# Weight narrowing on dense buffers, w_out's forms in w_in's ring, and both halves of the later batches' scores in one PSUM bank

## The chip, the cores and the metric

The kernel runs on one core of a Trainium2 chip. Its time is device microseconds (us) for one execution, taken as the median of several runs; the profile is of one further execution. Five engines run in parallel, each in its own order of instructions: TensorE (PE, with its weight loads shown apart as PEld), VectorE (DVE), ScalarE (ACT), GpSimd (POOL) and SyncE (SP), which here issues all DMAs. Matmuls write into PSUM, which has eight banks of 512 float32 columns for each of 128 partitions; everything else lives in SBUF.

## The reference

Channel attention for four batches, and a feed-forward network behind it:

```
B, N, C = 4, 6080, 256;  d_ff = 2048
qn = q / (norm(q, axis=1) + 1e-6);  kn = k / (norm(k, axis=1) + 1e-6)
s  = kn.transpose(0, 2, 1) @ qn / tau            # (B, 256, 256)
a  = exp(s - max);  a /= a.sum(-1) + 1e-9
x  = (v @ a).reshape(B * N, C)                   # 24320 tokens
h  = x @ w_in;  g = 0.5 * h * (1 + erf(h / sqrt(2)));  out = g @ w_out
```

Inputs are float32; the two weight matrices arrive as float64, which the kernel sees as pairs of 32-bit words.

## The kernel before, in words

The attention matrix is multiplied into w_in for each batch, so that a batch's tokens go through two matmul layers only. Every large product is made in a split form: each operand is a high part in a rounded 32-bit type (float32r) and a low part that is the rest, and three matmuls (high by high, low by high, high by low) are added in PSUM. Both layers also use a Strassen-like scheme of seven products of quarter blocks in the place of eight, for which sums and differences ("forms") of the weights and of the tokens are made.

**The stages.** (1) The scores of batch 0 in plain float32. (2) Eight rounds of `pair_out` and `plain_products` over the first pair of chunks of batch 0, while the remaining weights are narrowed from float64. (3) 184 steps, one for each chunk of up to 512 tokens and each of four groups of 512 hidden columns. A step runs seven products into the banks pa, pb, px and pz (`do`, L903 to L905), gelu on ACT twice (once rounded into `his`, L933, once whole into `gs`, L930), the low part on DVE into `los` (L936, L954), and the products with w_out of the step before it (L1020 to L1022 and L1036 to L1038) into the four banks po0 to po3.

**The scores of batches 1 to 3** are made inside the steps of the batch before. Every third step holds a "burst": four blocks of 128 tokens of k and q, already split into `hl`, are multiplied for the two halves m of the 256 k channels. In `burst` (L470) a half takes the whole spare bank: 512 columns in one pass hold k's high part by q's high part in columns 0 to 255 and by q's low part in columns 256 to 511, and a second pass of 256 columns adds k's low part by q's high part. `burst_sum` (L480) adds the bank's 512 columns to the running sum `sacc` in SBUF, once for each half; `softmax` (L623) adds the two halves of `sacc` together at its start (L636). There are 34 bursts. The first eight blocks of batch 1 go through `qk_fill` at the start.

**Narrowing** (`narrow`, L518) turns 512 pairs of words for each partition into a high and a low float32r array. The two words of a pair lie next to each other, so each 32-bit half is read with a step of two. L532 clamps the upper words and writes them back in place; L534 squares them on ACT; L537 and L539 shift the exponent bits, the second one again in place; L541 masks small values; L544 writes a power of two into the upper words; L545 multiplies the lower words by it; L547 (ACT), L548 and L549 make the high and the low part. Of the sixteen units five are narrowed in the first 70 us and eleven in stage 2, on two scratch tiles in turn, `kqc` and `osb`.

**w_out's forms** (`wo_forms`, `wo_adds`, `wo_hi`, `wo_lo`, L586 to L615) are made once for each of the four groups, in the first four steps: four sums into `osb` (L598), four more (L601 to L604), the high part of these on ACT (L608) and the low part on DVE (L612), in two pieces. One piece is written into `kqc`; the other goes into the front half of the same `osb` tile. Both are sent to DRAM by DMA (L614, L615) and read back later. There is one `osb` tile, so the next group's sums wait until the DMA has read it.

**What sets the order.** PE's order is written out by hand. ACT's, DVE's and SP's is set when the kernel is built by `Order` (L79): a list planner with a fixed price for each instruction runs the program 24 times on paper and keeps the order with the earliest end. Any change of an instruction, a buffer or a wait can move others far from it. Each engine then runs strictly in that order: an instruction that waits holds up everything behind it.

## Time and profile before

| | |
|---|---|
| median of 3 runs | 2061.69 us (2061.46 to 2065.83) |
| the profiled execution's own time | 2062.65 us |
| its span, first to last instruction | 2060.9 us |
| PE, PEld, DVE, ACT busy | 99%, 95%, 90%, 79% |
| weight loads and matmuls | 15958 each |

A matmul of 256 columns stays in the array for 275 ns, but the next one starts after 0.11 us, so "busy" says only that PE had work in flight. Lost time on PE shows in two ways: as idle time before a matmul, with what ended it, and as a granted clock under 1. Line numbers are those of the kernel before; "gs<-px" is the tile written and the tile read, and `p` is the tile p5, whose number the profile leaves out.

### The profile page before, as it was taken

How to read it: one execution, taken by the hardware profiler on the slowest of the kernel's cores; microseconds unless marked ns; L12 is line 12 of the kernel's file. 1: busy time of each engine (PE TensorE's matmuls, PEld its weight loads, DVE VectorE, ACT ScalarE, POOL GpSimd, SP SyncE). 2: the span in 40 equal slices, each digit the busy share in tenths (PEclk: the TensorE clock that was granted, in tenths of full speed). 3: DMA queues.
4: the chain of work that ended last, by engine and by line, in shares of the span. 5: the costliest groups of instructions: out<-in, count | busy, mean ns of one | idle time of the engine just before them, and what ended most of it. 6: DMA issues, size and time to landing. Idle time of an engine off the chain costs nothing.

```text
span 2060.9 us, 40753 instructions
## 1 busy us (share of the span) xinstructions
PE 2032.2 (99%) x15958; PEld 1962.3 (95%) x15958; DVE 1857.9 (90%) x2733; ACT 1620.7 (79%) x2720; POOL 1.3 (0%) x8
## 2 busy tenths in 40 slices
PE   8899999999999999999999999999999999999999
PEld 7778999999999999999999999999999999999999
DVE  6899899899899989999989999999998998898897
ACT  6666788888888888888988877777787777777776
POOL 0000000000000000000000000000000000000000
PEclk9999999999999999999999999999999999999999
DMA  9556687877787778687678666666556566566664
GB/s 376 177 187 220 225 277 239 270 262 258 245 298 253 244 252 273 223 279 257 225 267 267 206 225 225 215 211 213 198 185 224 177 200 214 189 202 206 199 196 166
DMA packets 153808, 475.31 MB, mean 231 GB/s; under 512 B 16016, under 2 KB 26256, under 8 KB 153104
## 3 DMA queue, kind: packets, MB, share of 16 engines
q1 hardware_dynamic: 153616, 472.71, 68.3%
q8 instruction: 125, 2.05, 0.4%
q14 instruction: 67, 0.55, 0.1%
HBM read 435.16 MB, written 37.49 MB: 229 GB/s over the span
## 4 chain that ended last, share of the span: by engine, by line
PE 87%; DVE 6%; DMA 3%; ACT 2%; issue 1%; SPq 0%; DVEq 0%; ACTq 0%
PE po L1038 10%; PE po L1037 10%; PE po L1036 10%; PE pb L903 5%; PE pb L904 5%; PE pb L905 5%; PE pa L903 5%; PE pa L904 5%; PE pa L905 5%; PE po L1020 4%; PE po L1022 4%; PE po L1021 4%; DMA raw<-qk 2%; PE pz L904 2%; PE pz L905 2%; PE pz L903 2%
## 5 line engine op out<-in xcount | busy, mean ns | idle before, releaser
L1038 PE MATMUL po<-los,wo 128*128 128x256 f32 (+1 forms) x1890 | 520.3, 275 | 0.8 <-DVE los L954 0.8
L1036 PE MATMUL po<-his,wo 128*128 128x256 f32 (+1 forms) x1890 | 520.4, 275 | 0.0
L1037 PE MATMUL po<-his,wo 128*128 128x256 f32 (+1 forms) x1890 | 519.9, 275 | 0.0
L936 DVE TENSOR_TENSOR los<-gs,his 128x512 fp32r<-128x512 f32 (+1 forms) x601 | 407.0, 682 | 67.9 <-ACT gs L930 53.4
L1036 PEld LDWEIGHTS po<-his,wo 128*128 128x128 f32 x1890 | 362.7, 192 | 1.9
L1038 PEld LDWEIGHTS po<-los,wo 128*128 128x128 f32 x1890 | 362.9, 192 | 1.3 <-DVE los L954 1.2
L1037 PEld LDWEIGHTS po<-his,wo 128*128 128x128 f32 x1890 | 362.9, 192 | 0.5
L954 DVE TENSOR_TENSOR los<-gs,his 128x1024 fp32r<-128x1024 f32 (+1 forms) x270 | 326.6, 1210 | 18.2 <-ACT his L950 16.6
L950 ACT CAST his<-gs 128x1024 fp32r<-128x1024 f32 (+1 forms) x270 | 281.2, 1043 | 75.3 <-DVE gs L947 73.2
L903 PE MATMUL pa<-vhi,wl 128*128 128x256 f32 (+1 forms) x920 | 253.3, 275 | 4.7 <-DVE pz L917 4.4
L903 PE MATMUL pb<-vhi,wl 128*128 128x256 f32 (+1 forms) x920 | 253.6, 276 | 3.1 <-ACT gs L930 1.3
L904 PE MATMUL pa<-vhi,wh 128*128 128x256 f32 (+1 forms) x920 | 253.2, 275 | 0.0
L905 PE MATMUL pa<-vlo,wh 128*128 128x256 f32 (+1 forms) x920 | 253.2, 275 | 0.0
L905 PE MATMUL pb<-vlo,wh 128*128 128x256 f32 (+1 forms) x920 | 253.1, 275 | 0.0
L904 PE MATMUL pb<-vhi,wh 128*128 128x256 f32 (+1 forms) x920 | 253.1, 275 | 0.0
L943 DVE TENSOR_TENSOR gs<-gs 128x1024 f32<-128x1024 f32 (+1 forms) x135 | 163.7, 1213 | 29.8 <-ACT gs L930 26.2
L903 PEld LDWEIGHTS pa<-vhi,wl 128*128 128x128 f32 x920 | 176.2, 191 | 9.9 <-DVE pz L917 5.8
L903 PEld LDWEIGHTS pb<-vhi,wl 128*128 128x128 f32 x920 | 176.3, 192 | 6.9 <-ACT his L933 1.5
L933 ACT ACTIVATE his<-px 128x512 fp32r<-128x512 f32 (+1 forms) x184 | 108.8, 591 | 90.7 <-PE px L905 88.6
L904 PEld LDWEIGHTS pa<-vhi,wh 128*128 128x128 f32 x920 | 176.3, 192 | 3.6
L904 PEld LDWEIGHTS pb<-vhi,wh 128*128 128x128 f32 x920 | 176.3, 192 | 2.4
L905 PEld LDWEIGHTS pa<-vlo,wh 128*128 128x128 f32 x920 | 176.8, 192 | 0.0
(284 smaller groups left out, 5138.7 us busy)
## 6 DMA issues: line engine op xcount, KB each, us to landing
wo<-keep_out SPq DMA_DIRECT2D x503, 512.0 KB, 4.5
raw<-qk SPq DMA_DIRECT2D x95, 512.0 KB, 6.1
kqc<-kqt SPq DMA_DIRECT2D x72, 512.0 KB, 5.1
wo<-keep_out SPq DMA_DIRECT2D x135, 256.0 KB, 4.0
v_raw<-vt SPq DMA_DIRECT2D x40, 512.0 KB, 6.6
out<-osb SPq DMA_DIRECT2D x40, 512.0 KB, 5.1
win<-keep_in SPq DMA_DIRECT2D x24, 512.0 KB, 6.1
keep_in<-win SPq DMA_DIRECT2D x4, 1024.0 KB, 4.4
```

The costliest lines, as they stand in the source:

```text
L903: nc.tensor.matmul(o, wls[g][:, a, q], paired(vh[:, at, :h]), start=start, stop=False, skip_group_check=True)
L904: nc.tensor.matmul(o, whs[g][:, a, q], paired(vh[:, at, :h]), start=False, stop=False, skip_group_check=True)
L905: nc.tensor.matmul(o, whs[g][:, a, q], paired(vl[:, at, :h]), start=False, stop=stop, skip_group_check=True)
L933: nc.scalar.activation(out=slot(name)[0], in_=t[SOURCE[name]], func=AF.Gelu)
L936: tt(out=slot(name)[1], in0=whole(name), in1=f32(slot(name)[0]), op=ALU.subtract)
L943: tt(out=g4[:, 0:2], in0=g4[:, 1:3], in1=g4[:, 0:2], op=ALU.subtract)
L950: nc.scalar.copy(out=views[1][:, 2 - 2 * i:4 - 2 * i], in_=views[0][:, 2 * i:2 * i + 2])
L954: tt(out=views[2][:, at], in0=views[0][:, 2 * i:2 * i + 2], in1=f32(views[1][:, at]), op=ALU.subtract)
L1020: nc.tensor.matmul(o, w[:, 1, q], mh, start=start, stop=False, skip_group_check=True)
L1036: nc.tensor.matmul(o, w[:, 1, q], mh, start=starts and q == 0, stop=False, skip_group_check=True)
L1037: nc.tensor.matmul(o, w[:, 0, q], mh, start=False, stop=False, skip_group_check=True)
L1038: nc.tensor.matmul(o, w[:, 0, q], ml, start=False, stop=stops and q == 1, skip_group_check=True)
```

## The change

Three things are changed.

1. *Narrowing in stage 2.* The upper words go into a dense array at the first instruction (L532) and stay there: for the units on `kqc` into the tile `p5`, for those on `osb` into a third row of that tile. All instructions that read or wrote the upper words with a step of two in the loaded pairs now use the dense array, except the first one's read; the lower words are still read in place, once. The five units of the first 70 us keep the old buffers.

2. *w_out's forms.* The high and low parts go into one tile of w_in's ring (`win`, two buffers) in place of `kqc` and the front half of `osb`. ACT's copy and DVE's subtraction are one instruction each over 1024 elements, where there were two over 512. The DMAs are of the same size and number.

3. *Scores.* Both halves m of a burst go into one bank, 256 columns each, in three passes of 256 columns for each block, where there were one of 512 and one of 256. A burst has 24 matmuls in the place of 16 (272 more in all, with as many weight loads). `sacc` is 512 columns wide for both halves together; DVE adds the bank once for each burst, after the second half. `softmax` reads `sacc` directly, with a step of two, in the multiplication that applies the norms (L672), and the additions of L636 are gone, as is a clearing on POOL.

Two places in the planned order follow, one on DVE and one on ACT. The first is DVE at the last of w_out's four sets of forms, in the fourth of the 184 steps. L598 to L612 (before) are the forms' instructions, L917 is the sum into the bank pz that PE's next products wait for. Before:

```order
L936 TENSOR_TENSOR los<-gs,his 128x512
L598 TENSOR_TENSOR osb<-wo 128x256 x3
L601 TENSOR_TENSOR osb<-osb 128x256
L602 TENSOR_TENSOR osb<-osb 128x256
L603 TENSOR_TENSOR osb<-osb 128x256
L598 TENSOR_TENSOR osb<-wo 128x256
L604 TENSOR_TENSOR osb<-osb 128x256
L612 TENSOR_TENSOR osb<-osb 128x2x256
L917 TENSOR_TENSOR pz<-pa,p_1838 128x512
L612 TENSOR_TENSOR kqc<-osb,kqc 128x2x256
```

And with the change, where the same lines are numbered 1 to 3 higher (L601 sums w_out's blocks, L604 to L607 make the forms, L613 the low part, L918 the sum into pz):

```order
L613 TENSOR_TENSOR win<-osb,win 128x4x256
L937 TENSOR_TENSOR los<-gs,his 128x512
L601 TENSOR_TENSOR osb<-wo 128x256 x2
L918 TENSOR_TENSOR pz<-pa,p_1843 128x512
L601 TENSOR_TENSOR osb<-wo 128x256
L604 TENSOR_TENSOR osb<-osb 128x256
L605 TENSOR_TENSOR osb<-osb 128x256
L606 TENSOR_TENSOR osb<-osb 128x256
L601 TENSOR_TENSOR osb<-wo 128x256
L607 TENSOR_TENSOR osb<-osb 128x256
L921 TENSOR_TENSOR p_1843<-pa,p_1843 128x512
```

The sum into pz stood behind nine of the forms' instructions and now stands behind two of them, and what frees `osb` is the DVE instruction L613 two rows ahead, where it was a DMA.

The second place is ACT at the two exponentials of batch 2's softmax (L680 before). ACT holds one function table at a time, and a table load stands ahead of each change between gelu and Exp. Before:

```order
L1062 COPY osb<-po_11402 128x512
L680 ACT_TABLE_LOAD
L680 ACTIVATE e_11758,small<-t_11417,small 128x256
L933 ACT_TABLE_LOAD
L933 ACTIVATE his<-px 128x2x240
L930 ACTIVATE gs<-px 128x2x240
L933 ACTIVATE his<-p_11744 128x2x240
L930 ACTIVATE gs<-p_11744 128x2x240
L933 ACTIVATE his<-pz 128x2x240
L930 ACTIVATE gs<-pa 128x2x240
L930 ACTIVATE gs<-pz 128x2x240
L680 ACT_TABLE_LOAD
```

With the change (L681 is the exponential, L914 and L836 are copies that need no table of their own):

```order
L1063 COPY osb<-po_11529 128x512
L681 ACT_TABLE_LOAD
L681 ACTIVATE e_11883,small<-t_11757,small 128x256
L914 COPY p_11869<-pb 128x2x240
L681 ACTIVATE e_11885,small<-t_11760,small 128x256
L836 CAST vhi<-vs 128x2x240
L934 ACT_TABLE_LOAD
L934 ACTIVATE his<-px 128x2x240
```

The two exponentials stand together between one pair of table loads. The same holds for batch 3; the whole program has 17 table loads where it had 21. The square root of batch 1's norms, which stood just ahead of that batch's exponentials, now stands 46 rows earlier in ACT's order.

The diff:

```diff
@@ -444,10 +444,9 @@
                     s[:, m], raw[:, j, 0, m * P:(m + 1) * P], raw[:, j, 1], start=(i == 0 and m == 0),
                     stop=(i == FILL * JS - 1), skip_group_check=True)
                 yield
-        acc = state["sacc"] = pm.tile([P, NCT, NT], F32, name="sacc")
-        nc.gpsimd.memset(acc[:, :, C:], 0.0)
+        acc = state["sacc"] = pm.tile([P, NCT, C], F32, name="sacc")
         for m in range(NCT):
-            nc.vector.tensor_copy(out=acc[:, m, 0:C].rearrange("p (b a) -> p b a", a=2), in_=paired(s[:, m]))
+            nc.vector.tensor_copy(out=acc[:, m].rearrange("p (b a) -> p b a", a=2), in_=paired(s[:, m]))
 
 
     def sum_up(nps, acc, start, stop):
@@ -469,22 +468,21 @@
 
     def burst(b, k, m):
         cs = slice(m * P, (m + 1) * P)
-        s = state["burst"] = spare()
-        ops = [(hls[b, k * NB + t], j) for t in range(NB) for j in range(JS)]
-        for i, (hl, j) in enumerate(ops):
-            nc.tensor.matmul(s, hl[:, 0, j, 0, cs], hl[:, :, j, 1].rearrange("p h (a b) -> p h b a", a=2), start=(i == 0), stop=False,
-                             skip_group_check=True)
-            nc.tensor.matmul(s[:, 0:C], hl[:, 1, j, 0, cs], paired(hl[:, 0, j, 1]), start=False,
+        if m == 0:
+            state["burst"] = spare().rearrange("p (m c) -> p m c", m=NCT)
+        s = state["burst"][:, m]
+        ops = [(hls[b, k * NB + t], j, x) for t in range(NB) for j in range(JS) for x in ((1, 0), (0, 0), (0, 1))]
+        for i, (hl, j, (x, y)) in enumerate(ops):
+            nc.tensor.matmul(s, hl[:, x, j, 0, cs], paired(hl[:, y, j, 1]), start=(i == 0 and m == 0),
                              stop=(i == len(ops) - 1), skip_group_check=True)
 
-    def burst_sum(k, m):
+    def burst_sum(k):
         s = state.pop("burst")
         if k == 0:
-            if m == 0:
-                state["sacc"] = pm.tile([P, NCT, NT], F32, name="sacc")
-            nc.vector.tensor_copy(out=state["sacc"][:, m], in_=s)
+            state["sacc"] = pm.tile([P, NCT, C], F32, name="sacc")
+            nc.vector.tensor_copy(out=state["sacc"], in_=s)
         else:
-            acc = state["sacc"][:, m]
+            acc = state["sacc"]
             nc.vector.tensor_tensor(out=acc, in0=s, in1=acc, op=ALU.add)
 
     norms = {}
@@ -521,13 +519,18 @@
         n = raw.shape[1]
         low, high = raw[:, :, 0], raw[:, :, 1]
 
+        own = None
         if "filled" not in state:
             tmp = pst.tile([P, 2, n], F32, name="nt", bufs=2)
         else:
             state["nt"] = not state.get("nt")
-            tmp = pg.tile([P, 2, n], F32, name="kqc" if state["nt"] else "osb", bufs=1)
-
-        top = high.bitcast(F32)
+            if state["nt"]:
+                tmp, own = pg.tile([P, 2, n], F32, name="kqc", bufs=1), pg.tile([P, NT], F32, name="p5")
+            else:
+                tmp = pg.tile([P, 3, n], F32, name="osb", bufs=1)
+                own = tmp[:, 2]
+
+        top = high.bitcast(F32) if own is None else own
         body, w, tail = tmp[:, 0].bitcast(U32), tmp[:, 0], tmp[:, 1]
         nc.vector.tensor_scalar(out=top, in0=high.bitcast(F32), scalar1=TOP_MAX, scalar2=-TOP_MAX,
                                 op0=ALU.min, op1=ALU.max)
@@ -540,7 +543,7 @@
                                        op0=ALU.bitwise_and, op1=ALU.bitwise_or)
         nc.vector.scalar_tensor_tensor(out=w, in0=tail, scalar=TOP_MIN ** 2, in1=top, op0=ALU.is_ge, op1=ALU.mult)
 
-        body = high
+        body = topu
         nc.vector.tensor_scalar(out=body, in0=w.bitcast(U32), scalar1=0xFF800000, scalar2=None, op0=ALU.bitwise_and)
         nc.vector.scalar_tensor_tensor(out=tail, in0=low, scalar=2.0 ** -52, in1=body.bitcast(F32), op0=ALU.mult,
                                        op1=ALU.mult)
@@ -586,8 +589,8 @@
     def wo_forms(g):
         whole = pg.tile([P, 8 * H], F32, name="osb")
         x = whole.rearrange("p (s f q n) -> p s f q n", s=2, f=4, q=2)
-        hl = whole[:, 0:4 * H].rearrange("p (f h q n) -> p f h q n", f=2, h=2, q=2).bitcast(F32R)
-        return x, [pg.tile([P, 2, 2, 2, P], F32R, name="kqc", bufs=1), hl]
+        t = pw.tile([P, 2, NCT, NT], F32R, name="win", bufs=2)
+        return x, t.rearrange("p a b n -> p (a b n)").rearrange("p (f h q n) -> p f h q n", f=4, h=2, q=2)
 
     def wo_adds(g, x):
         fa, fs = x[:, 0], x[:, 1]
@@ -604,15 +607,12 @@
         tt(out=s4, in0=a12, in1=s2, op=ALU.subtract)
 
     def wo_hi(x, hl):
-        for i in range(2):
-            nc.scalar.copy(out=hl[i][:, :, 0], in_=x[:, 1, 2 * i:2 * i + 2])
+        nc.scalar.copy(out=hl[:, :, 0], in_=x[:, 1])
 
     def wo_lo(g, x, hl):
-        for i in range(2):
-            nc.vector.tensor_tensor(out=hl[i][:, :, 1], in0=x[:, 1, 2 * i:2 * i + 2], in1=f32(hl[i][:, :, 0]),
-                                    op=ALU.subtract)
-        nc.sync.dma_start(out=keep_out[g][:, 0:4:3], in_=f32(hl[0]))
-        nc.sync.dma_start(out=keep_out[g][:, 4:6], in_=f32(hl[1]))
+        nc.vector.tensor_tensor(out=hl[:, :, 1], in0=x[:, 1], in1=f32(hl[:, :, 0]), op=ALU.subtract)
+        nc.sync.dma_start(out=keep_out[g][:, 0:4:3], in_=f32(hl[:, 0:2]))
+        nc.sync.dma_start(out=keep_out[g][:, 4:6], in_=f32(hl[:, 2:4]))
 
 
     def preload(func, after):
@@ -627,14 +627,11 @@
         rk, nms, dens = (small[:, 16 + 2 * i:18 + 2 * i] for i in range(3))
         ts = []
         for m in range(NCT):
-            t = pm.tile([P, C], F32, name=f"t{m}")
             if first:
+                t = pm.tile([P, C], F32, name=f"t{m}")
                 nc.scalar.copy(out=t, in_=state["s"][m])
             else:
-                s = state["sacc"]
-                both = s[:, m].rearrange("p (h b a) -> p h a b", h=2, a=2)
-                nc.vector.tensor_tensor(out=t.rearrange("p (a b) -> p a b", a=2), in0=both[:, 0], in1=both[:, 1],
-                                        op=ALU.add)
+                t = state["sacc"][:, m]
             ts.append(t)
         nsum = state.pop("nsum")
         if first:
@@ -669,8 +666,12 @@
         if not first:
             yield
         for m in range(NCT):
-            nc.vector.scalar_tensor_tensor(out=ts[m], in0=ts[m], scalar=rk[:, m:m + 1], in1=rq[:, 0:C],
-                                           op0=ALU.mult, op1=ALU.mult)
+            t, x, o = ts[m], rq[:, 0:C], ts[m]
+            if not first:
+                o = ts[m] = pm.tile([P, C], F32, name=f"t{m}")
+                t = t.rearrange("p (b a) -> p a b", a=2)
+                x, o = (y.rearrange("p (a b) -> p a b", a=2) for y in (x, o))
+            nc.vector.scalar_tensor_tensor(out=o, in0=t, scalar=rk[:, m:m + 1], in1=x, op0=ALU.mult, op1=ALU.mult)
             nc.vector.reduce_max(out=nms[:, m:m + 1], in_=ts[m], axis=AX.X, negate=True)
         yield
         es = []
@@ -1243,7 +1244,8 @@
             w = (4 if b == 1 else 3) + 3 * k
             for m in range(NCT):
                 put(n0 + w, "PE", burst, b, k, m)
-                put(n0 + w, "PEdve", burst_sum, k, m)
+            put(n0 + w, "PEdve", lambda: None)
+            put(n0 + w, "PEdve", burst_sum, k)
             for i in range(NB):
                 js = k * NB + i
                 put(max(0, n0 + w - 4 + i), "load", load_qk, b, js)
```

## The prediction

> **What bounds the kernel now.** I read the page's first part, the stretches of time, and then the waits of PE one by one in the timeline.
>
> ```profile
> span 2060.9 us, 40753 instructions
> PE 2032.2 (99%) x15958; PEld 1962.3 (95%) x15958; DVE 1857.9 (90%) x2733; ACT 1620.7 (79%) x2720; POOL 1.3 (0%) x8
> ```
>
> ```profile
> core 0: us, PE busy (x) PEld busy (x) DVE busy (x) ACT busy (x) POOL busy (x), PEclk, DMA share, GB/s
> 75.00:225.00 150.00, 141.75 (x742) 124.25 (x742) 140.64 (x245) 101.05 (x176) 0.00 (x0) 0.98 0.61 199
> 225.00:500.00 275.00, 275.00 (x2263) 269.26 (x2263) 251.62 (x348) 230.75 (x386) 0.00 (x0) 1.00 0.78 261
> 500.00:550.00 50.00, 48.13 (x387) 46.26 (x386) 45.23 (x82) 47.08 (x83) 0.00 (x0) 1.00 0.71 237
> 800.00:850.00 50.00, 48.25 (x380) 46.39 (x380) 45.82 (x73) 42.16 (x72) 0.00 (x0) 1.00 0.77 255
> ```
>
> ```profile
> 125.00:150.00 25.00, 22.83 (x97) 18.93 (x96) 24.55 (x42) 17.86 (x30) 0.00 (x0) 0.93 0.62 204
> 200.00:225.00 25.00, 22.00 (x137) 20.13 (x137) 21.36 (x40) 16.84 (x31) 0.00 (x0) 0.93 0.75 249
> ```
>
> From 225 us on PE is the bound: 275 us of 275 without a gap. There DVE's 251.6 us and ACT's 230.8 us run beside it, and relieving them gives nothing. The stretch from 75 to 225 us is different: PE idles 150.00 - 141.75 = 8.25 us, and in two windows the granted clock is 0.93, so 0.07 x 25 = 1.75 us of clock is lost in each. Between 125 and 150 us DVE is busy 24.55 of 25. So DVE sets the pace of the narrowing, and PE's waits there show it:
>
> ```profile
> 104.85 0.48 PE L981 MATMUL po<-his,wo 128*128 128x512 f32 x1 [0.31 <-DVE wo L549]
> ...
> 116.08 0.48 PE L981 MATMUL po<-his,wo 128*128 128x512 f32 x1 [0.60 <-DVE wo L549]
> ...
> 129.27 0.48 PE L729 MATMUL pa<-win,eh 128*128 128x512 f32 x1 [2.17 <-DVE win L549]
> 129.59 0.38 PE L730 MATMUL pa<-win,el 128*128 128x512 f32 x1
> ...
> 130.14 0.63 PE L729 MATMUL px<-win,eh 128*128 128x512 f32 x1
> 130.57 0.63 PE L730 MATMUL px<-win,el 128*128 128x512 f32 x1
> ...
> 170.68 0.38 PE L903 MATMUL pa<-vhi,wl 128*128 128x256 f32 x1 [0.43 <-DVE pz L917]
> ...
> 187.66 0.48 PE L1022 MATMUL po<-los,wo 128*128 128x512 f32 x1 [1.74 <-DVE los L936]
> ...
> 218.10 0.38 PE L903 MATMUL pa<-vhi,wl 128*128 128x256 f32 x1 [3.00 <-DVE pz L917]
> ```
>
> Three waits are for the last instruction of a narrowed unit (L549), three for DVE's low parts or sums. They add to 8.25 us. A wait costs more than its idle time. PE's pipe drains: a matmul of 512 columns lasts 0.38 us while the next may start after 0.21 us (129.59 to 129.80, the start before the clock drops), so some 0.16 us more, and the first one after a wait lasts 0.48 in the place of 0.38; together 0.26 us for each wait. And after the wait of 2.17 us matmuls start 0.43 us apart (130.14, 130.57), half speed; the window's clock puts that at 1.75 us, and the wait of 3.00 us has the same in its window. Total at stake: 8.25 + 6 x 0.26 + 2 x 1.75 = 13.3 us.
>
> [...]
>
> **The change part by part. Narrowing.** The rows of stage 2, and those of the same work elsewhere:
>
> ```profile
> L539 DVE SCALAR_TENSOR_TENSOR raw<-raw,kqc 128x512 uint32<-128x512 uint32 x6 | 5.4, 892 | 0.1
> L541 DVE SCALAR_TENSOR_TENSOR kqc<-kqc,raw 128x512 f32<-128x512 f32 x6 | 5.0, 838 | 0.1
> L545 DVE SCALAR_TENSOR_TENSOR kqc<-raw 128x512 f32<-128x512 uint32 x6 | 5.0, 829 | 0.0
> L537 DVE TENSOR_SCALAR kqc<-raw 128x512 uint32<-128x512 uint32 x6 | 3.3, 546 | 0.1
> L544 DVE TENSOR_SCALAR raw<-kqc 128x512 uint32<-128x512 uint32 x6 | 3.1, 516 | 0.0
> L548 DVE TENSOR_TENSOR kqc<-kqc,wo 128x512 f32<-128x512 f32 x4 | 2.8, 688 | 0.0
> ```
>
> ```profile
> L544 DVE TENSOR_SCALAR raw<-nt x3: 420/421/431, 13.8 to 54.5; 128x512 uint32<-128x512 uint32 x3
> ...
> L541 DVE SCALAR_TENSOR_TENSOR nt<-nt,raw x3: 683/691/693, 12.1 to 53.7; 128x512 f32<-128x512 f32 x3
> ...
> 75.00:129.20 54.20, 4.76 (x7) 1.00 0.52 164
> ```
>
> With the upper words in step two, two-input instructions take 829 to 892 ns; L548, as long and dense, takes 688 in the same stretch. In the first 55 us the same stepped L541 took 691 (minimum, median and maximum in the second fence), so the step costs only where PE runs at full rate, which is where the eleven units are. I take dense for L539 and L541 as 688: 204 + 150 ns less. L537 and L544 become dense on both sides, taken as L544's undisturbed 421: 125 + 95 less. L545 still reads the lower words in step two: between 0 and 141 less, taken as 70. The clamp (L532) still reads pairs: nothing. Sum 0.64 us for a unit; bounds 0, if a dense array meets the same disturbance, and 0.72. ACT's square gets denser too, but ACT waits for DVE here.
>
> Seven units end by 129.2 us (the last row counts L549): DVE is then 7 x 0.64 = 4.5 us earlier. To remove the first three waits it must be 0.31 + 0.60 + 2.17 and two restarts of 0.26 earlier, 3.6 us. So they go. PE is then 3.6 + 0.26 + 1.75 = 5.6 us ahead and DVE only 4.5: up to 1.1 us can come back as short waits for the gelu's low parts, until all eleven units (7.0 us) also cover the wait at 170.68 (0.43 + 0.26). At stake 3.51 + 4 x 0.26 + 1.75 = 6.3 us; I take 5.3.
>
> **w_out's forms.** The two late waits lie behind them:
>
> ```profile
> 182.58 1.10 DVE L598 TENSOR_TENSOR osb<-wo 128x256 f32<-128x256 f32 x3 [0.33 <-DMA out<-osb]
> ...
> 186.32 1.28 DVE L936 TENSOR_TENSOR los<-gs,his 128x512 fp32r<-128x512 f32 x2
> ...
> 213.62 1.10 DVE L598 TENSOR_TENSOR osb<-wo 128x256 f32<-128x256 f32 x3 [1.32 <-DMA keep_out<-osb]
> ...
> 217.35 0.69 DVE L917 TENSOR_TENSOR pz<-pa,p 128x512 f32<-128x512 f32 x1
> ```
>
> At 213.62 DVE has stood 1.32 us for the DMA that reads `osb`, then does 3.7 us of forms, and only then (217.35) the sum into pz that PE has wanted since 215. With the change `osb` is free as soon as DVE's own subtraction ends, and the new order puts the sum behind two forms' sums, not nine instructions. At 182.58 the first set still waits for an output DMA, but the low parts that PE waits for at 187.66 no longer follow the whole set: the planned order puts two of them before its first instruction. At stake 1.74 + 3.00 + 2 x 0.26 + 1.75 = 7.0 us; I take 6.5 (bounds 0, where another DMA holds DVE at the same places, and 7.0). Longer single instructions in place of halves, 1024 elements for twice 512, save DVE some 0.1 us a set and cost nothing.
>
> **Bursts.** A half of a burst and six passes of 256 columns elsewhere:
>
> ```profile
> 258.52 0.38 PE L475 MATMUL pb<-hl 128*128 128x512 f32 x1
> ...
> 259.83 0.38 PE L1020 MATMUL po<-his,wo 128*128 128x512 f32 x1
> ...
> 604.91 0.28 PE L903 MATMUL pa<-vhi,wl 128*128 128x256 f32 x1
> ...
> 605.59 0.28 PE L1036 MATMUL po<-his,wo 128*128 128x256 f32 x1
> ```
>
> Before, a half of eight passes takes 1.31 us (258.52 to 259.83). Six passes of 256, each with its own weight load, take 0.68 us, so twelve take 1.345 us: 0.035 us more for each of 68 halves, 2.3 us. PE is the bound there, so all of it counts (bounds 0 and 5, the starts being rounded to 0.01 us).
>
> On DVE 34 of the 68 additions go:
>
> ```profile
> L488 DVE TENSOR_TENSOR sacc<-pb,sacc 128x512 f32<-128x512 f32 x34 | 23.3, 685 | 1.1 <-PE pb L477 1.0
> L475 PEld LDWEIGHTS pa<-hl 128*128 128x128 f32 x136 | 25.8, 190 | 3.2 <-DVE sacc L485 0.3 <-ACT p L913 0.2
> ```
>
> That is 34 x 0.685 = 23 us off an engine that PE does not wait for there: nothing on the path. The step-two read of `sacc` is softmax's, some 0.1 us beside idle room.
>
> **Planned order.** The stalls after 225 us sit around softmax, where ACT is late with gelu because of table loads:
>
> ```profile
> 506.84 0.37 PE L903 MATMUL pb<-vhi,wl 128*128 128x240 f32 x1 [1.12 <-ACT his L933]
> ...
> 824.33 0.38 PE L903 MATMUL pb<-vhi,wl 128*128 128x256 f32 x1 [1.25 <-ACT gs L930]
> ...
> L680 ACT ACT_TABLE_LOAD x6 | 7.7, 1283 | 0.1
> ```
>
> The windows from 500 and from 800 us, shown first, hold 1.87 + 1.75 = 3.6 us of idle PE. Four of 21 loads of 1.28 us go, and batch 1's square root moves away from its exponentials, but the rest stands in new places. I take 2 us of gain; bounds a gain of 5, with the restarts, and a loss of as much.
>
> Sum: -5.3 - 6.5 + 2.3 - 2.0 = -11.5 us. The profiled execution took 2062.65 us around its span of 2060.9, 1 us over the median: span 2049.4, median 2061.7 - 11.5 = 2050.2 us.
>
> **The rivals.** *Dense arrays do not help.* The slow rows may come from the lower words, ACT or PE rather than from the step. Then the narrowing's 5.3 us stay lost: 2050.2 + 5.3 = 2055.5 us. The undisturbed 691 of a stepped L541 speaks for it, the 688 of dense L548 in the disturbed stretch against. [...] Chance 0.12.
>
> *The stalls move.* The planner's prices gave an order that waited 1.32 us for a DMA at 213.62; the new order can meet another such place. One more stall like that one (3.00 + 0.26 + 1.75 = 5.0), half of the narrowing's gain lost (2.7) and no gain around softmax (2.0): 2050.2 + 9.7 = 2059.9 us. Chance 0.12.
>
> *Slower: the one addition comes late.* The bank of a burst must be empty before the next step's first product. DVE, 251.6 of 275 us busy, now empties it in one go after the second half, and the planner may put it late. If PE waits 0.3 + 0.26 us at each of 34 bursts, 19 us come on top: 2069 us. From (11.5 + 4.1) / 34 = 0.46 us a burst it decides. Against it: the second half's addition had the same deadline before, and the waits for such additions are 0.3 us in all (L485 above). Chance 0.06.
>
> **How the numbers follow.** The forecast has 0.70, with a range of its own of 2044 to 2056 (terms at their bounds, not all at once). A measurement here can tell 0.2%, 4.1 us, from no change. Faster, under 2057.6: nearly all of the forecast (0.69), most of the first rival (0.08), a little of the second (0.02): 0.79. Slower: the last rival and 0.01 for the others: 0.07. Same: 0.14. The range of 8 in 10 runs from 2043 to 2060.
>
> **What would show it.** L539's and L541's successors at 680 to 700 ns and the first products with the seventh unit without the wait of 2.17 us; no half clock at 130 and 218 us; no wait for a DMA before the forms' sums; twelve passes in 1.34 us; 17 table loads. Wrong it would be if the dense rows stay over 800 ns, if PE idles for more than 3 us between 75 and 225 us, or if the windows behind 225 us, where PE had no gap, show waits for the burst's addition.

## The result, and the profile after

The changed kernel takes 2050.15 us (median of 4 runs, 2049.11 to 2051.99), the kernel before 2063.76 us beside it (4 runs, 2061.46 to 2067.07). The ratio is 0.9934, with a 95% interval of 0.9915 to 0.9952: about 0.7% faster. The profiled execution took 2049.57 us. Two later measurements of the same kernel gave the ratio 0.9934 (0.9921 to 0.9948) and 0.9935 (0.9922 to 0.9947).

The first lines of the changed kernel's page:

```profile
span 2047.7 us, 41220 instructions
PE 2030.2 (99%) x16230; PEld 1970.7 (96%) x16230; DVE 1832.7 (90%) x2689; ACT 1609.4 (79%) x2712; POOL 0.8 (0%) x7
```

PE has 272 more matmuls, yet is busy 2.0 us less and the span is 13.2 us shorter: what went is idle time and time at half clock. The stretches of time of the changed kernel say where (columns as before: stretch and length, then busy us of PE, PEld, DVE, ACT, POOL, then the granted clock, DMA share, GB/s):

```profile
75.00:225.00 150.00, 148.61 (x854) 133.74 (x853) 140.96 (x248) 111.82 (x196) 0.00 (x0) 1.00 0.66 219
125.00:150.00 25.00, 23.61 (x107) 19.74 (x107) 24.56 (x44) 16.77 (x30) 0.00 (x0) 1.00 0.59 188
200.00:225.00 25.00, 25.00 (x198) 24.20 (x197) 22.94 (x37) 21.27 (x36) 0.00 (x0) 1.00 0.91 307
225.00:500.00 275.00, 274.52 (x2303) 269.67 (x2302) 249.83 (x357) 230.99 (x388) 0.00 (x0) 1.00 0.77 263
500.00:1050.00 550.00, 548.59 (x4549) 537.95 (x4548) 498.97 (x724) 468.31 (x795) 0.00 (x0) 1.00 0.76 256
1050.00:2040.00 990.00, 989.54 (x8240) 972.47 (x8240) 887.11 (x1271) 754.53 (x1271) 0.00 (x0) 1.00 0.62 207
```

PE's idle time between 75 and 225 us fell from 8.25 to 1.39 us, and the clock of 0.93 in two windows is 1.00. DVE is busy there as long as before (140.96 against 140.64 us), with more of PE's work done in the same time (854 matmuls against 742). The counterparts of the last two rows in the kernel before:

```profile
500.00:1050.00 550.00, 545.91 (x4437) 532.29 (x4436) 503.11 (x741) 471.04 (x795) 0.00 (x0) 1.00 0.75 253
1050.00:2040.00 990.00, 988.83 (x8120) 968.37 (x8120) 896.72 (x1295) 763.56 (x1284) 0.00 (x0) 1.00 0.63 210
```

So 4.09 us of idle PE between 500 and 1050 us became 1.41 and 1.17 us behind it became 0.46, against which 0.48 us of new idle time stands between 225 and 500 us. Two waits are left in stage 2, in PE's timeline:

```profile
125.55 0.48 PE L730 MATMUL pa<-win,eh 128*128 128x512 f32 x1 [0.52 <-DVE win L552]
...
129.22 0.48 PE L982 MATMUL po<-his,wo 128*128 128x512 f32 x1 [0.86 <-DVE wo L552]
```

L552 is the old L549, the last instruction of a narrowed unit. The wait of 2.17 us has become 0.52, and PE now waits 0.86 us for the unit behind it.

The narrowing's instructions on DVE in stage 2, grouped by line (the six units on `kqc`, whose dense upper words are the tile `p`):

```profile
L542 DVE SCALAR_TENSOR_TENSOR p<-p,kqc 128x512 uint32<-128x512 uint32 x6 | 4.1, 680 | 0.4 <-ACT kqc L537 0.4
L544 DVE SCALAR_TENSOR_TENSOR kqc<-kqc,p 128x512 f32<-128x512 f32 x6 | 4.1, 688 | 0.1
L548 DVE SCALAR_TENSOR_TENSOR kqc<-raw,p 128x512 f32<-128x512 uint32 x6 | 4.9, 820 | 0.0
L540 DVE TENSOR_SCALAR kqc<-p 128x512 uint32<-128x512 uint32 x6 | 2.6, 425 | 0.1
L547 DVE TENSOR_SCALAR p<-kqc 128x512 uint32<-128x512 uint32 x6 | 2.5, 422 | 0.0
```

The old L539, L541, L537 and L544 took 892, 838, 546 and 516 ns on these six units; they take 680, 688, 425 and 422. The old L545, which still reads the lower words in step two, stays at 820 (829 before).

DVE at the fourth set of w_out's forms, in the timeline (L601 is the sums of w_out's blocks, L918 the sum into pz):

```profile
203.80 1.22 DVE L613 TENSOR_TENSOR win<-osb,win 128x1024 fp32r<-128x1024 f32 x1 [0.23 <-ACT win L610]
...
205.54 0.75 DVE L601 TENSOR_TENSOR osb<-wo 128x256 f32<-128x256 f32 x2
206.42 0.70 DVE L918 TENSOR_TENSOR pz<-pa,p 128x512 f32<-128x512 f32 x1
```

No DMA is waited for, and the sum that PE wants follows two sums of the forms. Neither wait, 1.74 nor 3.00 us, is left in PE's rows.

A half of a burst in PE's timeline:

```profile
251.20 1.50 PE L476 MATMUL pb<-hl 128*128 128x256 f32 x12
252.54 0.38 PE L1021 MATMUL po<-his,wo 128*128 128x512 f32 x1
```

Twelve passes take 1.34 us from first start to the next product's start. The exponentials have four table loads where they had six; ACT's rows hold 17 in all.

### The profile page after: what moved, and what is told of

Same layout as the page of the kernel before. It is cut to its first block, busy times and chain, and to the rows that moved or that the text cites. A ratio compares the mean times of both kernels' runs of the same rounds, so it can differ in the third digit from the quotient of the medians.

```text
span 2047.7 us, 41220 instructions
## 1 busy us (share of the span) xinstructions
PE 2030.2 (99%) x16230; PEld 1970.7 (96%) x16230; DVE 1832.7 (90%) x2689; ACT 1609.4 (79%) x2712; POOL 0.8 (0%) x7
## 4 chain that ended last, share of the span: by engine, by line
PE 92%; DVE 4%; DMA 2%; ACT 1%; issue 1%; SPq 0%; DVEq 0%; ACTq 0%
PE po L1039 10%; PE po L1038 10%; PE po L1037 10%; PE pb L906 5%; PE pb L904 5%; PE pb L905 5%; PE pa L905 5%; PE pa L906 5%; PE pa L904 5%; PE po L1021 4%; PE po L1023 4%; PE po L1022 4%; PE pb L476 2%; PE pa L476 2%; PE pz L906 2%; PE pz L905 2%
## 5 line engine op out<-in xcount | busy, mean ns | idle before, releaser
L906 PEld LDWEIGHTS pb<-vlo,wh 128*128 128x128 f32 x920 | 176.6, 192 | 0.0
```

The lines of the kernel that those rows point to most:

```text
L906: nc.tensor.matmul(o, whs[g][:, a, q], paired(vl[:, at, :h]), start=False, stop=stop, skip_group_check=True)
```

## The experiments

Each kernel was timed beside the kernel before on the same chip, which took a median of 2061.87 us beside the first four, 2062.35 us beside the next four and 2064.06 us beside the last two.

### The three parts, one at a time

**Narrowing alone.** Only the narrowing is on dense arrays. SP's planned order is that of the kernel before. DVE's and ACT's isn't quite, though that was expected: between 77 and 155 us some instructions stand earlier or later among the others. But ahead of the last instruction of the seventh unit, the one that PE waits for at 129 us in the kernel before, DVE runs the same instructions in both kernels.

```diff
-            tmp = pg.tile([P, 2, n], F32, name="kqc" if state["nt"] else "osb", bufs=1)
+            if state["nt"]:
+                tmp, own = pg.tile([P, 2, n], F32, name="kqc", bufs=1), pg.tile([P, NT], F32, name="p5")
+            else:
+                tmp = pg.tile([P, 3, n], F32, name="osb", bufs=1)
+                own = tmp[:, 2]
-        top = high.bitcast(F32)
+        top = high.bitcast(F32) if own is None else own
...
-        body = high
+        body = topu
```

> Only the narrowing is moved to dense buffers; forms and scores stay as before. The planner's prices depend on element counts alone, so DVE, ACT and SP keep the order of before. My theory (shorter DVE instructions in the DVE-bound stretch): the stepped instructions fall from 829-892 to about 685 ns, the waits of 0.31, 0.60 and 2.17 us for narrowed units shrink to 1.7 us or less in all, half clock at 130 us goes, and the span is 4 to 6 us shorter than before. The two waits behind w_out's forms (1.74 and 3.00 us before) stay within 0.7 us of that. Rival (the gain came from the planner's new order): under 1 us. Rival (a shorter square on ACT is what helps): DVE rows shorten but PE's waits for L549's successor stay.

Measured: 2057.61 us, ratio 0.9976 (0.9966 to 0.9986); 4.3 us faster, in the profiled span 5.4. From this kernel's stretches and PE's timeline:

```profile
75.00:175.00 100.00, 98.18 (x482) 85.09 (x481) 96.16 (x170) 68.73 (x123) 0.00 (x0) 1.00 0.63 202
175.00:225.00 50.00, 45.79 (x304) 42.38 (x303) 43.64 (x81) 31.98 (x57) 0.00 (x0) 0.97 0.66 223
```

```profile
181.85 0.48 PE L1027 MATMUL po<-los,wo 128*128 128x512 f32 x1 [1.32 <-DVE los L941]
...
212.18 0.46 PE L908 MATMUL pa<-vhi,wl 128*128 128x256 f32 x1 [2.89 <-DVE pz L922]
```

Stage 2 has lost its long wait, while the two waits at the forms stay, 1.32 and 2.89 us, with the half clock after the second. The last instruction of the seventh unit starts at 124.19 us, before at 128.53: 4.3 us earlier, of which 0.7 us were there at 69 us already, ahead of stage 2's units. The other 3.7 us are the narrowing's own: with the same instructions ahead, their order can't have brought them.

**Forms alone.**

```diff
-        hl = whole[:, 0:4 * H].rearrange("p (f h q n) -> p f h q n", f=2, h=2, q=2).bitcast(F32R)
-        return x, [pg.tile([P, 2, 2, 2, P], F32R, name="kqc", bufs=1), hl]
+        t = pw.tile([P, 2, NCT, NT], F32R, name="win", bufs=2)
+        return x, t.rearrange("p a b n -> p (a b n)").rearrange("p (f h q n) -> p f h q n", f=4, h=2, q=2)
```

> Only w_out's forms go to w_in's ring. My theory (a DMA no longer holds DVE, and the sum into pz leaves the tail of the forms): the waits of 1.74 and 3.00 us and the half clock behind the second go, 5 to 7 us; the wait of 2.17 us at 129 us stays. Rival (another DMA holds DVE at the same place): DVE still stands over 1 us before the forms' sums and the gain is under 2 us.

Measured: 2055.47 us, ratio 0.9964 (0.9952 to 0.9977); 6.4 us faster. Its stretches, and PE's timeline in stage 2:

```profile
75.00:175.00 100.00, 95.57 (x456) 81.87 (x456) 98.64 (x165) 69.52 (x121) 0.00 (x0) 0.99 0.53 172
175.00:225.00 50.00, 50.00 (x346) 47.01 (x345) 44.64 (x80) 40.17 (x70) 0.00 (x0) 1.00 0.83 279
```

```profile
128.75 0.48 PE L726 MATMUL pa<-win,eh 128*128 128x512 f32 x1 [2.30 <-DVE win L549]
...
132.60 0.48 PE L978 MATMUL po<-his,wo 128*128 128x512 f32 x1 [0.97 <-DVE wo L549]
```

Here it is the other way round: between 175 and 225 us PE has no gap, and stage 2 keeps its wait of 2.30 us. So the two parts remove different waits. Whether the forms gain by the DMA no longer holding `osb` or by the place of the sum in the order isn't told apart by this kernel: both came with the one edit. The kernel with the scores alone, whose forms are the old ones, says something about it. Its third set of forms, from 201.54 us, meets no DMA wait, and yet PE stands for the sum behind it:

```profile
206.10 0.38 PE L902 MATMUL pb<-vhi,wl 128*128 128x256 f32 x1 [1.93 <-DVE pz L916]
```

So the sum's place costs PE close to 2 us without any DMA. In the kernel before, 3.00 - 1.32 = 1.7 us of the long wait are left when the DMA's share is taken off. By these rows both have a part, the place the larger one; a kernel with only one of them changed wasn't tried.

**Scores alone.** The diff's edits of `burst`, `burst_sum`, `softmax` and the fill; narrowing and forms as before.

```diff
-        s = state["burst"] = spare()
-        ops = [(hls[b, k * NB + t], j) for t in range(NB) for j in range(JS)]
+        if m == 0:
+            state["burst"] = spare().rearrange("p (m c) -> p m c", m=NCT)
+        s = state["burst"][:, m]
+        ops = [(hls[b, k * NB + t], j, x) for t in range(NB) for j in range(JS) for x in ((1, 0), (0, 0), (0, 1))]
```

> Only the scores change: both halves in one bank, 256 columns a pass, softmax reads the sum directly. My theory: each of 68 halves takes 1.34 us in the place of 1.31, 1.8 us more; 17 table loads in the place of 21 and other places for the stalls take 3 to 4 us off behind 225 us; the stretch from 75 to 225 us keeps its 8 us of idle PE; together 1 to 3 us faster. Rival (relief of DVE by 34 additions is worth as much as the rest): 6 us or more faster. Rival (the passes cost more than they show): slower by 1 us or more.

Measured: 2063.35 us against 2061.87, ratio 1.0 (0.9991 to 1.0009): no change, where one to three microseconds of gain had been expected. This kernel's stretch behind stage 2 and the forms, with the same stretch of the kernel before below it:

```profile
225.00:1050.00 825.00, 821.87 (x6851) 806.65 (x6851) 744.93 (x1072) 702.06 (x1186) 0.00 (x0) 1.00 0.77 258
```

```profile
225.00:1050.00 825.00, 820.91 (x6698) 801.56 (x6698) 754.73 (x1088) 701.80 (x1180) 0.00 (x0) 1.00 0.76 256
```

DVE is busy 9.8 us less and PE idles 3.1 us in the place of 4.1. The additions taken off DVE show no gain in time. PE waits for DVE little there in any case, 1.8 us in all behind 225 us in the kernel before, and these waits didn't go (2.7 us here); and the burst's longer passes take back what the softmax gives.

**All but the narrowing** (forms and scores).

```diff
-            if state["nt"]:
-                tmp, own = pg.tile([P, 2, n], F32, name="kqc", bufs=1), pg.tile([P, NT], F32, name="p5")
-            else:
-                tmp = pg.tile([P, 3, n], F32, name="osb", bufs=1)
-                own = tmp[:, 2]
+            tmp = pg.tile([P, 2, n], F32, name="kqc" if state["nt"] else "osb", bufs=1)
```

(This and the other removal are against the changed kernel.)

> The changed kernel with the old narrowing. If the parts add, it is slower than the changed kernel by what the narrowing alone gains over the kernel before, 4 to 6 us, about 2055 us. If the narrowing's gain is covered by slack that the other parts make, the difference is under 2 us.

Measured: 2055.44 us, ratio 0.9964 (0.9951 to 0.9978). PE's long wait in its stage 2:

```profile
129.11 0.48 PE L725 MATMUL pa<-win,eh 128*128 128x512 f32 x1 [2.24 <-DVE win L547]
```

The wait of 2.24 us is back without the dense arrays. Against the changed kernel, 2050.15 us, the narrowing is worth 5.3 us on top of the other two; alone it was worth 4.3. The two kernels were timed on different occasions. By their gains over the kernel before beside each, 13.6 and 6.4 us, it is worth 7.2. So its size on top of the others is known only to within 2 us.

**All but the scores** (narrowing and forms), beside the changed kernel measured again on the same chip.

```diff
-            put(n0 + w, "PEdve", lambda: None)
-            put(n0 + w, "PEdve", burst_sum, k)
+                put(n0 + w, "PEdve", burst_sum, k, m)
```

> The narrowing and w_out's forms without the change of the scores. If the scores' change is worth nothing beside the other two (2.0 us less of stalls against 1.8 us more of passes), it takes 2049 to 2052 us, within 1.5 us of the changed kernel. If its additions on DVE help once the other parts are in, it is 3 us or more slower than the changed kernel.

> The changed kernel itself, for a comparison on the same chip as the two runs before it: 2049 to 2052 us.

Measured: 2050.23 us (ratio 0.9939, 0.9927 to 0.9952) and, for the changed kernel, 2048.92 us (ratio 0.9934, 0.9921 to 0.9948). The stretch behind 225 us, first without the scores, then with them:

```profile
225.00:1050.00 825.00, 820.74 (x6682) 801.25 (x6681) 754.97 (x1093) 698.98 (x1177) 0.00 (x0) 1.00 0.76 257
```

```profile
225.00:1050.00 825.00, 823.23 (x6856) 807.96 (x6855) 749.03 (x1081) 699.87 (x1183) 0.00 (x0) 1.00 0.76 258
```

With the scores PE idles 1.8 us there, without them 4.3: the 2.5 us are seen in the profile. The intervals of the two times overlap almost wholly, so the net of 1.3 us isn't settled.

### Is it the step, or working in place in the loaded pairs?

The dense arrays differ from the old ones in two ways: no step of two, and no writing into the tile that the DMA filled. In this kernel the five units on `osb` get an array of their own that is read and written in step two; the six on `kqc` stay dense.

```diff
-                tmp = pg.tile([P, 3, n], F32, name="osb", bufs=1)
-                own = tmp[:, 2]
+                whole = pg.tile([P, 4, n], F32, name="osb", bufs=1)
+                tmp = whole[:, 0:2]
+                own = whole[:, 2:4].rearrange("p a (c w) -> p (a c) w", w=2)[:, :, 0]
```

> The changed kernel, with one thing put back: the five narrowed units on osb keep their upper words in a step of two, in a part of the same scratch tile, not in the loaded pairs. The six units on kqc stay dense, and so do order and waits. If the step itself costs time while PE runs at full rate, the instructions of the osb units (L542, L544, L547's places) take 830 to 890 and some 515 ns again, those of the kqc units 690 and 425. If the cost came from working in place in the loaded pairs (beside the DMA that fills the ring), both sets take 690 and 425.

Measured, from a single execution: 2050.68 us, against 2062.35 for the kernel before. The groups of lines on DVE in stage 2 (lines are one higher than in the changed kernel; `osb` is the stepped kind, `kqc` and `p` the dense one):

```profile
L543 DVE SCALAR_TENSOR_TENSOR osb<-osb 128x512 uint32<-128x512 uint32 x5 | 4.3, 854 | 0.1
L543 DVE SCALAR_TENSOR_TENSOR p<-p,kqc 128x512 uint32<-128x512 uint32 x6 | 4.2, 704 | 0.3 <-ACT kqc L538 0.3
L545 DVE SCALAR_TENSOR_TENSOR osb<-osb 128x512 f32<-128x512 f32 x5 | 4.3, 860 | 0.0
L545 DVE SCALAR_TENSOR_TENSOR kqc<-kqc,p 128x512 f32<-128x512 f32 x6 | 4.3, 710 | 0.1
```

The same instructions in the same stretch take 150 ns more with the step, with no loaded pair written. The tile isn't the reason: in the changed kernel the five units on `osb` take 685 and 683 ns for these two lines. The order isn't either, since DVE and ACT run their instructions in the changed kernel's order. It is the step, and it reaches PE: its two waits left in stage 2, 0.52 and 0.86 us in the changed kernel, are 1.52 and 1.03 us here. (The dense rows are 22 to 24 ns above the changed kernel's; why isn't known.)

### What is left: the half clock at 69 us

After all three edits the largest loss between 60 and 225 us is a wait of 4.14 us at 69.40, with the clock at half behind it (0.50 from 67.70 to 74.53 us). In this kernel the fifth unit is narrowed in stage 2 and not ahead of that wait:

```diff
-        if len(units) in (11, 12):
+        if len(units) == 12:
-    paces = (2, 2, 1, 2, 2, 1, 1)
+    paces = (3, 2, 1, 2, 2, 1, 1)
-    for _ in range(3):
+    for _ in range(2):
```

(The last pair of lines stands at two places, the loading and the narrowing of the first units.)

> The changed kernel with the fifth weight unit narrowed after batch 0's softmax, in the planned part, not before it. In the changed kernel PE waits 4.14 us at 69 us for the first split of the weights, which stands behind that unit on DVE, and then runs ten matmuls at half clock. Theory: the wait falls under 1.5 us and the half clock goes, DVE fills the 3.2 us in which it waited for a load at 71 to 75 us; 3 to 5 us faster than the changed kernel, about 2046 us. Rival: the stretch behind it is bound by DVE all the same, the unit's 7 us of DVE come back there as waits of PE, and the time stays at 2050 us.

Measured: 2049.41 us, ratio 0.9936 (0.9924 to 0.9949), beside 2048.92 for the changed kernel: no gain. The first row is the changed kernel's wait and the second this kernel's; the third is this kernel's stretch around it, and the last a new wait:

```profile
69.40 0.80 PE L848 MATMUL pa<-vhi,wl 128*128 128x512 f32 x1 [4.14 <-DVE wl L722]
```

```profile
67.80 0.48 PE L848 MATMUL pa<-vhi,wl 128*128 128x512 f32 x1 [3.02 <-DVE wl L722]
...
60.00:75.00 15.00, 11.56 (x51) 9.17 (x51) 13.98 (x27) 10.52 (x21) 0.00 (x0) 1.00 0.65 226
...
1007.43 0.44 PE L694 MATMUL pa<-ident,e 128*128 128x128 f32 x2 [1.48 <-ACT e L681]
```

The wait is 1.1 us shorter and the clock stays whole, but the planner's new order makes PE stand 1.48 us for an exponential at 1007 us. The last kernel is this one with softmax's transposes one step later, so that this wait can't arise:

```diff
-                        (41, "PE"), (41, "PEact"), (41, "PEdve")):
+                        (42, "PE"), (42, "PEact"), (42, "PEdve")):
```

> The changed kernel with the fifth unit narrowed late, as in the run before, and softmax's transposes one step later in the PE order. In that run PE gained 2 us before 225 us and lost 1.6 us to the transposes of batch 2, which waited for an exponential. Theory: that wait goes, the time is 2 to 4 us under the changed kernel's. Rival: the new planned order puts stalls of the same size elsewhere, and the time is the changed kernel's within 1.5 us.

> The changed kernel itself, on the same chip as the run before it: 2048 to 2051 us.

Measured: 2049.96 us (ratio 0.9929, 0.9916 to 0.9943) and the changed kernel 2050.44 us (ratio 0.9935, 0.9922 to 0.9947). The two can't be told apart. In this kernel's profile the wait at 1007 us is gone, but the clock in the stretch from 60 to 75 us is lower again, after a wait of the same length:

```profile
67.53 0.48 PE L848 MATMUL pa<-vhi,wl 128*128 128x512 f32 x1 [3.02 <-DVE wl L722]
...
60.00:75.00 15.00, 11.89 (x44) 9.20 (x45) 12.70 (x25) 9.38 (x19) 0.00 (x0) 0.89 0.66 235
```

Between 225 and 1050 us PE still idles 2.4 us, now in short waits of at most 0.5 us. No version was found that beats the changed kernel.

## Why the prediction was right

The forecast was 2050.2 us and the measurement 2050.15. That the two agree to 0.05 us is luck. The forecast was a gain of 11.5 us from a median of 2061.7; the measured gain is 13.6 us from 2063.76, and 13.4 and 13.6 us in the two later measurements. So the prediction was short by 2 us of gain, and the kernel before, with one run more, came out 2 us above the base that it had taken. Here are the terms, with the gains of each part by medians:

| term | predicted | measured |
|---|---|---|
| narrowing | -5.3 | -4.3 alone, -5.3 to -7.2 on top of the others |
| forms | -6.5 | -6.4 alone |
| bursts and planned order | +0.3 | +1.5 alone, -1.3 on top of the others, neither told from 0 |

The gains alone add to 9.2 us and not to 13.6, so single terms are known only to a microsecond or two.

**Narrowing: right in mechanism, about right in size.** On the six units on `kqc`, whose rows the prediction read, L539 and L541 lost 212 and 150 ns (predicted 204 and 150), L537 and L544 121 and 94 (125 and 95). L545 lost 9 (829 to 820 ns), not the 70 I took between 0 and 141: with the one stepped input that it has left it stayed as slow. The clamp, costed at nothing, gave 40 ns for writing densely:

```profile
L535 DVE TENSOR_SCALAR p<-raw 128x512 f32<-128x512 f32 x6 | 3.0, 504 | 3.2 <-DMA raw<-w_out 3.2
```

(504 ns against 544 for the old L532.) The sum is 212 + 150 + 121 + 94 + 9 + 40 = 626 ns for such a unit, predicted 0.64 us; two errors cancel. The five units on `osb` had less to win, because their old rows were lower: 156 + 139 + 90 + 90 + 27 + 35 = 537 ns in the same order of lines. Eleven units make 6.4 us, where the prediction had 7.0. The rival that dense arrays don't help is refuted by these rows and by the stepped scratch array. ACT's square got shorter as well (934 to 630 ns on `kqc`, 929 to 641 on `osb`); that wasn't separated from DVE's part, and DVE's own rows are enough to carry the sum.

The prediction let up to 1.1 us of short waits come back. 0.52 + 0.86 us did, but in front of narrowed units and not, as it said, in front of gelu's low parts. They are all of the 1.39 us of idle time left between 75 and 225 us, so the wait at 170.68 is covered, as predicted.

**The half clock at 130 us cost little by itself.** The 1.75 us at stake there were read from the window's clock of 0.93 and added to the sum in full. But the next thing that PE needs is another narrowed unit. Three profiles with the same long wait and full clock behind it (forms alone, scores alone, all but the narrowing) show a second wait of about 1 us in front of the product that is L981 in the kernel before, 0.97 us in the row quoted for forms alone. The kernel before, at half clock, had none there: it arrived later. From the end of the long wait to that product it took 133.43 - 129.27 = 4.16 us before, and 132.60 - 128.75 = 3.85 us with full clock:

```profile
133.43 0.38 PE L981 MATMUL po<-his,wo 128*128 128x512 f32 x1
```

So with full clock that product would have come 0.3 us earlier and not 1.75, and at 143 us the three kernels wait another 0.21 to 0.34 us that the kernel before doesn't. DVE set the pace in any case, and (last section) it ran faster while PE ran slower: 0.42 and 0.69 us for the two instructions behind the wait, against 0.57 and 0.77 with full clock. The half clock could be won only as far as DVE itself came earlier, and the prediction had bounded its term by that: up to 1.1 us of 6.3 were to come back. What came back is 1.39 us of waits and two restarts of 0.26, which leaves 4.4 us of the 5.3 taken. The trace before has the half clock, 0.50 from 129.88 to 133.29 us (last section), but little could have been won by a full clock alone.

**Forms: right.** 6.4 us against 6.5; no DMA wait, no idle PE between 175 and 225 us, no half clock.

**Bursts: about right, with a slip in the working.** Twice the 0.68 us read for six passes is 1.36 us and not 1.345, which would have made 3.4 us and not 2.3. Measured, the 68 halves take 1340 ns on the mean against 1313, 1.83 us in all.

**Planned order: about right.** Idle PE behind 225 us fell by 2.9 us (worked out below); predicted 2.0. The 17 table loads came as the order showed. The gain came with the scores' edit: without it PE idles 4.3 us between 225 and 1050 us, with it 1.8. Which of the changes in the order gave it wasn't isolated.

**The rivals.** *The stalls move* didn't happen here, but did in the kernel with the late unit: 1.48 us at 1007 us, from an edit that had nothing to do with it. It did with the scores alone, too, where PE idles 2.1 us between 225 and 500 us; the kernel before had no gap there. *The one addition comes late* didn't happen: behind 225 us no row of PE's waits names the burst's sum.

**The whole.** As an account of PE's own time (what a loss was worth by itself is another matter, as the half clock at 130 us shows), of the 13.2 us of span 6.9 are idle PE between 75 and 225 us, 1.0 the restarts of 0.26 that went with four waits fewer, 3.5 the two windows at half clock, and 2.68 - 0.48 + 0.71 = 2.9 the idle time behind 225 us; 1.8 go back to the bursts. That makes 12.5 us; 0.7 us are not assigned.

The same can be had without pricing restarts or clock. PE's order is the same in both kernels but for the bursts, so one product can be timed in both profiles. The one at 80.21 us before starts at 79.75 after, the one at 175.07 at 170.24, the one at 226.04 at 214.30. So the changed kernel is 0.5 us ahead at the first, 4.8 at the second, 11.7 at the third, and 13.2 at the end. The narrowing's stretch gave 4.4 us (predicted 5.3), the forms' 6.9 (6.5), all behind it a gain of 1.4, where the prediction had a loss of 0.3, and 0.5 us were there by 80 us, where the prediction had nothing. In single profiles a half clock that happens to come or not moves such numbers by a microsecond or two (3.41 us at half speed are 1.7 us).

## What to carry to other kernels

Where a group of equal instructions takes longer in one stretch than in another, look at the access pattern and at what else runs there before you count instructions: here a step of two cost nothing while PE stood or ran slowly (stepped 684 and 691 ns in the first 55 us, dense 680 and 688 in stage 2), and 0.1 to 0.2 us an instruction beside a PE at full rate. Price a stall, or a clock drop behind it, by what the waiting engine needs next; if the slow engine is late for that too, the loss is already paid for. And when a planner sets the order, any edit can be worth a microsecond or two in either direction somewhere else, so test the parts one by one before you credit them.

## What the runs showed of the hardware that was not expected

**A wait of two or three microseconds didn't always bring half clock: its place among windows of 3.41 us made the difference.** The kernel before dropped to half clock after 2.17 us. Waits of 2.30, 2.26 and 2.24 us at the same place in three other kernels didn't bring it. The wait of 3.02 us is the clearest: in two kernels that do the same work up to there, one kept the clock (1.00 in the stretch from 60 to 75 us) and the other lost it (0.89). After 4.14 us it was lost in each profile looked at for it.

The granted clock in the traces shows the difference. Within a trace it changed only at moments that lie whole multiples of 3.413 us apart: each half clock, but for those that the program's end cuts off, lasted 3.41 or 6.83 us, and the full clock between the two late ones of the kernel before lasted 85.33 us, 25 times 3.413. (The kernel before is at 0.50 from 68.44 to 75.27, from 129.88 to 133.29 and from 218.63 to 222.04 us, the changed kernel from 67.70 to 74.53.) Cut into windows at these moments, the kernel before (the first two rows) has its whole wait of 2.17 us in one window, and half clock in the next; with the forms alone (the last two) the wait of 2.30 us straddles a boundary, with 0.89 us of idle PE in one window and 1.40 in the other:

```profile
126.47:129.88 3.41, 1.24 (x6) 0.76 (x6) 3.41 (x7) 1.95 (x4) 0.00 (x0) 1.00 0.39 105
129.88:133.29 3.41, 3.41 (x10) 2.66 (x9) 3.34 (x7) 1.71 (x3) 0.00 (x0) 0.50 0.99 366
```

```profile
123.94:127.35 3.41, 2.52 (x12) 1.87 (x10) 3.41 (x7) 2.48 (x5) 0.00 (x0) 1.00 0.32 124
127.35:130.77 3.42, 2.02 (x9) 1.49 (x9) 3.39 (x7) 1.85 (x5) 0.00 (x0) 1.00 0.81 271
```

The two waits of 3.02 us differ in the same way: 1.76 and 1.36 us where the clock was kept, 2.80 us in one window where it was lost. Over the twelve profiles each of the 14 drops before the program's end follows a window with 2.17 us or more of idle PE, and of some 7000 other windows at full clock none has more than 1.81. In the kernel before the three drops follow windows with 3.03, 2.17 and 2.89 us of idle PE, in the changed kernel the one drop follows 2.44. So in these profiles a window didn't have to be idle all through: 2.17 us of 3.41 were enough, 1.81 were not. Where the windows lie differed from profile to profile: a boundary is at 129.88 us in the kernel before and at 127.35 with the forms alone, while the wait ended at 129.27 and at 128.75. A half clock in a single profile is thus not a term to count on.

**The price of a step of two went with PE's rate.** Before, the stepped L539 took 892 ns on the mean in stage 2 on `kqc`, and 872 in the median on `osb`, but the one instance that fell into PE's wait of 2.17 us took 0.68 us, and the two stepped instructions that fell into the half clock behind that wait were fast as well: 0.42 and 0.69 us, where the medians on `osb` are 524 and 864 ns. DVE's timeline of the kernel before:

```profile
127.93 0.68 DVE L539 SCALAR_TENSOR_TENSOR raw<-raw,osb 128x512 uint32<-128x512 uint32 x1
...
130.41 0.42 DVE L544 TENSOR_SCALAR raw<-osb 128x512 uint32<-128x512 uint32 x1
130.87 0.69 DVE L545 SCALAR_TENSOR_TENSOR osb<-raw 128x512 f32<-128x512 uint32 x1
```

And the same three instructions of the same unit in the kernel with the forms alone, where PE waits from about 126.4 to 128.75 us and then runs at full clock:

```profile
127.39 0.70 DVE L539 SCALAR_TENSOR_TENSOR raw<-raw,osb 128x512 uint32<-128x512 uint32 x1
...
129.85 0.57 DVE L544 TENSOR_SCALAR raw<-osb 128x512 uint32<-128x512 uint32 x1
130.46 0.77 DVE L545 SCALAR_TENSOR_TENSOR osb<-raw 128x512 f32<-128x512 uint32 x1
```

The first is fast in both, where PE stands. The other two take 150 and 80 ns more where PE's clock is full. Code, tiles and place are the same and PE's rate differs, so PE at full rate has a part in the price; by what way, these rows don't say. DMAs alone didn't make it: in the window at half clock, 129.88 to 133.29 us, their engines are busy for 0.99 of the time, and the stepped instructions in it are fast. It was PE's rate and not the clock as such: in the first 55 us the granted clock is 1.00, but the plain float32 products there start 0.22 us apart for 256 columns, as slowly as 512 columns in 0.43 us at half clock, and the stepped L541 takes 691 ns there. ACT was hit as well: in the experiment with the stepped scratch its square took 919 ns on the stepped array and 627 on the dense one:

```profile
L538 ACT ACTIVATE osb<-osb 128x512 f32<-128x512 f32 x5 | 4.6, 919 | 0.0
L538 ACT ACTIVATE kqc<-p 128x512 f32<-128x512 f32 x6 | 3.8, 627 | 1.6 <-DVE p L536 1.6
```

So reading and writing float32 words in a step of two cost nothing here while PE stood (0.68 us for L539, dense 680 ns) or ran at half clock (0.42 us for L544, dense 422 ns), and some 150 ns in 700 while it ran at full rate (854 and 860 ns against 704 and 710).
